# An attention and FFN kernel whose VectorE transposes start two pairs earlier, with twice as many pairs on float32 scores

## The chip, the cores and the metric

The kernel runs on one core of a Trainium2 chip. The metric is the device time of one launch in microseconds; the kernel before has a median of 1023.87 us over three runs (1023.54 to 1024.44). Five engines work side by side, each through its own queue in order: TensorE (PE, with its weight loads as PEld), VectorE (DVE), ScalarE (ACT), GpSimd (POOL) and SyncE (SP), which issues most DMAs. Matmuls write to eight PSUM banks.

## The reference

Attention with a decay over 8 batches, 8 heads, 576 positions and 64 dimensions, then a two-matrix feed-forward block over the 4608 tokens:

```python
scores = (q @ k.T) / 8                       # per batch and head, 576 x 576
cum    = cumsum(log(clip(f, 1e-4, 1)))       # 64 rows of 576
scores = where(causal, -1e9, scores + cum[:, None] - cum[None, :])
attn   = softmax(scores); o = attn @ v       # float32
h      = x @ w_in                            # x: 4608 x 512, w_in: 512 x 2048
g      = max(h, 0) + alpha * min(h, 0)
out    = g @ w_out                           # 2048 x 512
```

The term of a row's own position drops out of the softmax, so only the row of column sums, times -8, is added to the raw scores before the scaling by -1/8.

## The kernel before, in words

Two heads of a batch make a pair; there are 32 pairs, four to a batch. `attention(n)` writes down the work of pair n: loads, scores of four query tiles of 128 and a tail of 64 (heads on the two halves of TensorE's rows), a reduction on VectorE that adds the decay rows Z and takes the row's least value, an exponential on ScalarE, a transposition, the product with v (`values`), and the division by the sums (`rest`), which leaves x of the pair in two parts.

Scores come in two forms (`terms` in `load_n`). A pair below `NN` multiplies q and k in float32, one matmul for each piece. A later pair first splits q and k into a high and a low part (two copies on ScalarE, subtractions on POOL) and adds three products: Qh Kh, Qh Kl, Ql Kh.

Transposition also comes in two forms. A pair below `NX[0]` has its exponentials turned on TensorE in blocks of 128 against `ident` (L612), and ScalarE or VectorE carries them from PSUM to SBUF. A "turned" pair, from `NX[0]` on, has its exponentials laid out so that four VectorE transposes of 128 x 768 (L807) and 16 DMAs of 96 KB turn them; its k columns and its Z are permuted for that. The turned pairs use other cuts of the same SBUF (`big`, `wr`), which `swap` hands over.

Work that is not attention fills in: `load_w_in(fc)` turns one of 16 column groups of w_in into a high and a low part (`split64`: a square on ScalarE, L359, L360, L363 and L364 on VectorE in a scratch tile from the ring `rwa`, a copy on ScalarE, and two subtractions on POOL, L369), and `ffn1(b)` multiplies x of batch b with the 16 groups, 12 matmuls of 512 columns for each (all through the helper at L373), of which six need the first two pairs of the batch and six the other two. The rest of the first matrix and then the second one follow the last pair.

The order on each engine is set when the program is built. `op` records every step with an engine, a duration by a formula, a key, its dependencies and the buffers that it takes; `Plan.run` places them one by one at the earliest time that its own clock gives, lower keys first. So a table of constants moves instructions everywhere. Where the plan expects TensorE to stand, it puts matmuls of `ident` that nobody reads (`fill`, L470); a row of dummy matmuls on `wr` (L436) opens the program.

Of the kernel before, what the change touches and what calls it, by code (L numbers as in the profile page):

```python
# [18 lines left out]
NP = H // 2  # L19
# [7 lines left out]
NN = 4  # L27
# [7 lines left out]
NX = (10, B * NP)  # L35
# [14 lines left out]
LATE = (0, B - 1, B)  # L50

# [47 lines left out]
class Plan:  # L99
    def __init__(self):  # L100
        self.now = dict.fromkeys(ENGS, 0.0)
        self.chan = 0.0
        self.ops = []
        self.banks = self.fill = None

    def op(self, eng, ns, fn, key, deps=(), bufs=(), two=False, kb=0.0, glue=0.0, need=None):
        o = Op()
        o.glue, o.need = glue, need
        o.eng, o.ns, o.fn, o.key, o.bufs, o.two, o.kb = eng, ns / 1000.0 * SLACK.get(eng, 1.0), fn, key, bufs, two, kb
# [104 lines left out]
def attention_moe(  # L214
# [49 lines left out]
    rS, rT = Ring(banks, 2, 4), Ring(banks, 1, 3)  # L264
# [3 lines left out]
    rhs = Ring(Store([hs[:, i] for i in range(4)]))  # L268
# [16 lines left out]
    rT1 = Ring(Store(cuts_of(0, 3, 384)))  # L285
    re3, re = Ring(Store(cuts_of(1664, 1, 1024))), Ring(Store(cuts_of(2688, 3, S)))
# [5 lines left out]
    res = Ring(Store(cuts_of(1152, 2, 256) + [wf[:, 2560 + 256 * i : 2816 + 256 * i] for i in range(2)]))  # L292
# [9 lines left out]
    rwa = Ring(Store([wf[:, 2048:2560].bitcast(U32)]))  # L302
# [129 lines left out]

    o_wbf = op("DVE", 300, lambda: ve.memset(wbf, 1.0), -102)
    bw = Buf(rS)
    for i in range(7):
        op("PE", 800, lambda: [pe.matmul(bw.t, wbf[:, 0:128], wbf, start=True, stop=True) for _ in range(3)], -200, [o_wbf], [bw])  # L436
# [38 lines left out]
    def load_n(n, held):  # L475
# [5 lines left out]
        q_, k_ = (lambda: bqk.t[:, 0:QW]), (lambda: bqk.t[:, QW : QW + S])  # L481
        kq = -99 if first else -59 if n == 1 else kl
# [7 lines left out]
        Z, Zt = (lambda: bZ.t[0]), (lambda: bZ.t[1])  # L490
        rz = []
# [9 lines left out]
        for h in range(2):  # L501
            if spread:
                got = [zz]
            elif first:
                bz_ = Buf(rH)
                up = op("PE", 4 * c_mm(512), lambda h=h, bz_=bz_: mm(bz_.t, row()[:, h], ft()[:, 0:512], True, True), -60 + h, o_8 + [o_row], [bft, brow, bz_])
                got = [op("ACT", c_act(512), lambda h=h, bz_=bz_: ac.activation(Z()[:, h, 0:512], bz_.t, AF.Copy), -60, [up], [bz_, bZ])]
            else:
                c8_, o_ = (c8p, o_c8p) if n >= NX[0] else (c8, [o_c8])
                got = [op("SP", 400, lambda h=h, c8_=c8_: sy.dma_start(Z()[:, h, 0:512], c8_[bh + h : bh + h + 1, 0:512].broadcast_to([128, 512])),  # L510
                          kl + 1, o_, [bZ], kb=256)]
            if n >= NX[0]:
# [11 lines left out]
            tb = lambda k: tri.rearrange("p (k s) -> p k s", k=1).broadcast_to([128, k, 128])  # L524
            on, o_e, o_c = (ve, "DVE", c_dve) if first and h < FD else (po, "POOL", c_po)
# [3 lines left out]
            rz.append([m1, m2, m3])  # L529
        if spread:  # L530
            tz = [zt]
        elif first:
            bz2 = [Buf(rH), Buf(rH)]
            cut = ((0, 512), (512, S))

            def up2():
                for b_, (a0, a1) in zip(bz2, cut):
                    mm(b_.t[:, 0 : a1 - a0], row()[:, 2], ft()[:, a0:a1], True, True)

            up = op("PE", 4 * c_mm(512) + 440, up2, -58, o_8 + [o_row], [bft, brow] + bz2)  # L540
# [22 lines left out]
    waiting, behind, tails, later_x, quick_ops, value_ops = [], [], [], [], [], []  # L563

    def attention(n):
# [9 lines left out]
        turned = NX[0] <= n < NX[1]  # L575
        bv = Buf(rvr)
# [46 lines left out]
        def tail(st):  # L623

            nonlocal e4
            bt = bE if turned else Buf(re)
# [19 lines left out]
            if turned:  # L646
# [125 lines left out]
        def tile(h, i, st, bS, s, c0):  # L772

            nonlocal e4
            w = 128 * i + 128
# [25 lines left out]
            if turned:  # L801
# [12 lines left out]
                return  # L814
            if i == 1:
# [6 lines left out]
                t = op("PE", 3 * 109, tr1, st + 0.3, [be[h][0][1], nm, o_id], [bT, be[h][0][0], b1])  # L822
                e1[h] = evac(bT, 384, st + 0.3, [t], lambda: bT1[h].t, lambda: bT.t[:, :384], [bT1[h]])
            if i >= 2:
# [8 lines left out]
                t = op("PE", (i + 1 + last) * 109, tr2, st + 0.3, [nm, o_id] + ([nt] if last else []), [bT, b1] + ([bt] if last else []))  # L833
                to, tb = ((lambda: bT3.t[:, :, 192 * h : 192 * h + 128]), bT3) if i == 3 else ((lambda: bT2[h].t[:, 0:3, 0:128]), bT2[h])
# [48 lines left out]
        def rest():  # L883
            bx, xo = Buf(rx), []
# [38 lines left out]
        behind.append(values)  # L923
        if n == B * NP - 1:
# [3 lines left out]
        if n < NE - 1 or n in (NX[0] - 1, B * NP - 1):  # L928
            while behind:
                vb, vp, vd, done = behind.pop(0)()  # L930
                value_ops.append(op("PE", ns_v + 250, vp, k0 + 9.6 - hurry, vd, vb))
                done(value_ops[-1])
        if n >= NV2 and n % 2 == 0:
# [10 lines left out]
        elif not (n >= NV2 and n % 2 == 0):  # L944
# [3 lines left out]
            del later_x[:-keep]  # L948

# [65 lines left out]
    o_ct = [op("POOL", c_po(S) + 60, lambda h=h: sides(h), kc_ + 3, [o_cq]) for h in range(2)]  # L1015
    def swap():
        rS.most, rT.least, rH.most = 8, 0, 3
        for st, t in [(rE.store, big[:, 0:EW]), (rTT.store, big[:, EW + 3072 :]), (rTT.store, wf[:, 0:3072])] + [(rM.store, t) for t in cuts_of(EW, 4, 768)]:
            st.free.append((plan.t, len(st.items)))
            st.items.append(t)  # L1020

    op("-", 0, swap, 0, [value_ops[-1]] + [o for v in w_ready.values() for o in v])
# [300 lines left out]
```

## Time and profile before

| what | value |
|---|---|
| median of three runs | 1023.87 us (1023.54 to 1024.44) |
| profiled execution | 1022.34 us, its span 1020.5 us |
| busy in the span: PE, DVE, ACT, POOL | 1008.1, 803.6, 652.2, 389.5 us |
| mean granted TensorE clock | 0.998 of 2.4 GHz |
| chain of waits, share of PE | 94% |

The span runs from the first to the last instruction of one profiled execution. Busy times overlap, since the engines work side by side. A matmul's own time includes its way through the array, so the spacing of starts, not the mean duration, tells what one costs in a row of them.

### The profile page before, as it was taken

The page shows a single profiled execution, that of the slowest core. Times are in us where ns is not written, and L with a number is a line of the kernel's source. Part 1 is how long each engine was busy: PE and PEld are TensorE (multiplying, and loading weights), DVE is VectorE, ACT ScalarE, POOL GpSimd, SP SyncE. Part 2 cuts the span into 40 slices and gives each one's busy share as a digit, 9 for nine tenths or more (in the row PEclk, how much of TensorE's full clock was granted, in tenths as well). Part 3 has the DMA queues.
Part 4 walks back from the last instruction along what each step waited for, and adds up shares of the span by engine and source line. Part 5 has one row for each costly group of instructions (what it writes and reads, how often), then busy time and mean ns, then how long its engine had stood idle before and what let it go on. Part 6 is the DMA issues. An engine that isn't in the chain of part 4 may idle for free.

```text
span 1020.5 us, 22569 instructions
## 1 busy us (share of the span) xinstructions
PE 1008.1 (99%) x7932; PEld 889.0 (87%) x7932; DVE 803.6 (79%) x1727; ACT 652.2 (64%) x1550; POOL 389.5 (38%) x652
## 2 busy tenths in 40 slices
PE   9989989999999999999999999999999999999998
PEld 5778868888888888888888888899999999999998
DVE  6778875888887887857727976698998888989994
ACT  6979977677777777767634755555464645546551
POOL 6597983769877879758240000000000000000000
PEclk9999999999999999999999999999999999999999
DMA  6868764688888897887746674543443343434411
GB/s 197 245 187 264 241 192 124 184 229 263 264 256 250 240 260 217 257 239 208 203 140 222 208 232 164 196 146 125 134 134 126 124 145 125 136 113 145 131 57 42
DMA packets 126398, 187.88 MB, mean 184 GB/s; under 512 B 22135, under 2 KB 71790, under 8 KB 126286
## 3 DMA queue, kind: packets, MB, share of 16 engines
q1 hardware_dynamic: 121774, 173.27, 55.4%
q0 software_dynamic: 4224, 12.98, 4.8%
q8 instruction: 62, 1.02, 0.4%
q14 instruction: 50, 0.41, 0.1%
q10 hardware_dynamic: 288, 0.20, 0.1%
HBM read 102.95 MB, written 48.67 MB: 149 GB/s over the span
## 4 chain that ended last, share of the span: by engine, by line
PE 94%; POOL 3%; DVE 1%; DMA 1%; ACT 1%; issue 0%; SPq 0%; DVEq 0%; POOLq 0%
PE bank L373 90%; PE bank L612 2%; POOL wi L369 1%; PE bank L436 1%; DMA wr<-in_w_in_dram 1%; DMA ri<-rd 0%; PE bank L470 0%; POOL Z L519 0%; POOL Ql L558 0%; POOL Kl L558 0%; POOL xx L895 0%; DVE xs L891 0%; ACT big L608 0%; PE bank L691 0%; PE bank L651 0%
## 5 line engine op out<-in xcount | busy, mean ns | idle before, releaser
L373 PE MATMUL bank<-xx,wi 128*128 128x512 f32 x1728 | 410.5, 393 | 5.6 <-POOL wi L369 4.1
L373 PEld LDWEIGHTS bank<-xx,wi 128*128 128x128 f32 x1728 | 320.3, 188 | 74.7 <-POOL wi L369 5.0
L599 ACT ACTIVATE big<-big,st 128x384 f32<-128x384 f32 (+4 forms) x268 | 156.1, 585 | 22.2 <-DVE st L795 21.6
L795 DVE CUSTOM_DVE_ANT_0 big<-bank,Z 128x256 f32<-128x256 f32 (+3 forms) x211 | 92.2, 491 | 47.1 <-PE bank L373 42.6
L373 PE MATMUL bank<-wot,xx 128*128 128x256 f32 x1008 | 123.9, 283 | 0.0
L373 PE MATMUL bank<-wi,xx 128*128 128x256 f32 x1008 | 123.9, 283 | 0.0
L373 PEld LDWEIGHTS bank<-wi,xx 128*128 128x128 f32 x1008 | 122.3, 192 | 0.0
L373 PEld LDWEIGHTS bank<-wot,xx 128*128 128x128 f32 x1008 | 122.3, 192 | 0.0
L981 DVE SCALAR_TENSOR_TENSOR hs<-bank,sa,hs 128x512 f32<-128x512 f32 x96 | 71.6, 746 | 51.7 <-ACT hs L979 50.0
L979 ACT ACTIVATE hs<-bank,ab 128x512 f32<-128x512 f32 x96 | 65.9, 686 | 58.3 <-PE bank L373 56.6
L519 POOL TENSOR_TENSOR Z<-Z,tri 128x128 f32<-128x128 f32 x176 | 72.4, 443 | 46.5 <-DVE Z L497 42.5
L807 DVE STREAM_TRANSPOSE big<-big 128x768 f32<-128x768 f32 x88 | 81.1, 953 | 3.5 <-ACT big L599 3.5
L1207 ACT ACTIVATE xx<-gx 128x1024 fp32r<-128x1024 f32 x48 | 50.8, 1058 | 30.7 <-PE bank L373 13.4
L895 POOL TENSOR_TENSOR xx<-xs,xx 128x256 fp32r<-128x256 f32 x64 | 49.6, 792 | 47.5 <-ACT xx L893 47.0
L1210 DVE TENSOR_TENSOR xx<-gx,xx 128x1024 fp32r<-128x1024 f32 x48 | 58.5, 1219 | 7.9 <-ACT xx L1207 7.9
L373 PE MATMUL bank<-big,vr 128*64 128x128 f32 (+2 forms) x1136 | 62.7, 263 | 0.5 <-DVE st L640 0.3
L373 PE MATMUL bank<-wi,gh 128*128 128x256 f32 x504 | 62.4, 283 | 0.0
L373 PE MATMUL bank<-wot,gh 128*128 128x256 f32 x504 | 62.4, 283 | 0.0
L373 PEld LDWEIGHTS bank<-wot,gh 128*128 128x128 f32 x504 | 61.4, 192 | 0.1
L373 PEld LDWEIGHTS bank<-wi,gh 128*128 128x128 f32 x504 | 61.3, 192 | 0.0
L373 PEld LDWEIGHTS bank<-big,vr 128*64 128x64 f32 x1136 | 54.5, 137 | 7.9 <-issue 5.0
L373 PE MATMUL bank<-Kh,Qh 64*128 64x128 f32 (+2 forms) x280 | 58.7, 350 | 0.0
(161 smaller groups left out, 1747.9 us busy)
## 6 DMA issues: line engine op xcount, KB each, us to landing
hd<-hs SPq DMA_DIRECT2D x144, 256.0 KB, 3.9
wx<-hd SPq DMA_DIRECT2D x47, 512.0 KB, 3.4
rqk<-in_qk_dram SPq DMA_DIRECT2D x28, 512.0 KB, 6.1
hr<-hd SPq DMA_DIRECT2D x25, 512.0 KB, 4.7
big<-big SPq DMA_DIRECT2D x110, 96.0 KB, 2.8
wr<-big SPq DMA_DIRECT2D x110, 96.0 KB, 4.4
vr<-in_vv_dram SPq DMA_DIRECT2D x32, 320.0 KB
wr<-in_w_in_dram SPq DMA_DIRECT2D x16, 512.0 KB, 5.8
```

What stands on the lines that cost most here:

```text
L369: return [op("POOL", c_po(256), lambda h=h: po.tensor_tensor(wlo()[:, h], a()[:, h].bitcast(F32), whi()[:, h].bitcast(F32), ALU.subtract), ...
L373: pe.matmul(o, lhsT, rhs, start=start, stop=stop)
L519: ms.append(op("POOL", c_po(128), lambda to=to, i=i, zd=zd: po.tensor_tensor(to()[:, :, -1:], zd()[:, :, i : i + 1], tk(), ALU.add), kc + ...
L599: ex = op("ACT", c_exp(w), lambda: ac.activation(at(bt.t), at(bt.t), AF.Exp, bias=lo()[:, col : col + 1], scale=-1.0, accum_out=su()[:, co ...
L612: pe.transpose(t[:, c : c + 128], src[:, 128 * j : 128 * j + 128], ident)
L795: ve.tensor_tensor_reduce(out=o if turned else blk(o), in0=blk(bS.t[:, c0 : c0 + w]), in1=in1(), scale=-0.125, scalar=3.0e38, op0=ALU.add, ...
L807: tn = op("DVE", c_tr(768), lambda k=k: ve.transpose(part(bm[k].t), part(bE.t[:, 768 * k : 768 * k + 768])), k0 + TK + k / 10, done, [bE, ...
L895: xl = op("POOL", c_po(256), lambda r=r, t0=t0: po.tensor_tensor(bx.t[:, 1, t0 : t0 + 256], bxs[r].t[:, 0:256], bx.t[:, 0, t0 : t0 + 256]. ...
L979: cp = op("ACT", c_act(512), lambda bh=bh, bs=bs, fc=fc: ac.activation(bs.t, bh.t, AF.Relu, scale=ab[:, fc : fc + 1]), -1000, [last, o_sg] ...
L981: cp = op("DVE", c_dve(512), lambda bh=bh, bs=bs, fc=fc: ve.scalar_tensor_tensor(bs.t, bh.t, sa[:, fc : fc + 1], bs.t, ALU.mult, ALU.add), ...
L1207: his.append(op("ACT", c_acs(128 * GW * (j1 - j0)), lambda j0=j0, j1=j1, src=src, o_=o_: ac.activation(o_(0, j0, j1), src(), AF.Copy), key ...
L1210: rdy.append(op("DVE", c_dve(128 * GW * (j1 - j0)), lambda j0=j0, j1=j1, src=src, o_=o_: ve.tensor_tensor(o_(1, j0, j1), src(), o_(0, j0, ...
```

## The change

- `NX` starts at 8 instead of 10: pairs 8 and 9 become turned ones. Their Z is still loaded by DMA.
- `NN` is 8 instead of 4: pairs 4 to 7 take the float32 scores and are no longer split.
- The decay rows of the pairs that are not turned are kept in another arrangement, so that two additions of 256 columns for each head stand where an addition of 384, one of 128 and a copy of 128 stood. For pair 0 the two additions of one head read PSUM.
- The rows that are spread for pair 0 are the sums themselves, with -8 in the selecting matrix, instead of sums that VectorE has multiplied by -8. The selecting matrix has a place of its own (`rT1`) and is written earlier on POOL.
- Six of the 21 opening matmuls go.
- The score ring keeps four banks from the start and may hold six (two and four before).
- The scratch ring `rwa` of the w_in conversion has two tiles; the second is a fourth of `hs`, which `ffn1` gets back after the last conversion.
- SBUF is handed to the turned pairs in three steps (`swap`, `swap1`, `swap2`): after the last TensorE transposition, after the last value product before them, and after the last conversion. Other cuts of `big` move to suit.
- A table `SHIFT`, which is empty, could add to the keys.

```diff
-NN = 4
+NN = 8
-NX = (10, B * NP)
+NX = (8, B * NP)
...
-    rS, rT = Ring(banks, 2, 4), Ring(banks, 1, 3)
+    rS, rT = Ring(banks, 4, 6), Ring(banks, 1, 3)
...
-    rhs = Ring(Store([hs[:, i] for i in range(4)]))
+    rhs = Ring(Store([hs[:, i] for i in range(3)]))
...
-    rwa = Ring(Store([wf[:, 2048:2560].bitcast(U32)]))
+    rwa = Ring(Store([wf[:, 2048:2560].bitcast(U32), hs[:, 3].bitcast(U32)]))
...
-    brow = Buf(re)
+    brow = Buf(rT1)
...
-                po.affine_select(o, o, pattern=[[0, w]], base=-h, channel_multiplier=1, compare_op=ALU.not_equal, fill=1.0)
-
-    o_row = op("POOL", 1500, rows, -100, (), [brow])
+                po.affine_select(o, o, pattern=[[0, w]], base=-h, channel_multiplier=1, compare_op=ALU.not_equal, fill=-8.0)
+
+    o_row = op("POOL", 1000, rows, -101, (), [brow])
...
-    for i in range(7):
+    for i in range(5):
...
-                up = op("PE", 4 * c_mm(512), lambda h=h, bz_=bz_: mm(bz_.t, row()[:, h], ft()[:, 0:512], True, True), -60 + h, o_8 + [o_row], [bft, brow, bz_])
+                up = op("PE", 4 * c_mm(512), lambda h=h, bz_=bz_: mm(bz_.t, row()[:, h], cu()[:, 0:512], True, True), -60 + h, o_sc + [o_row], [bcu, brow, bz_])
...
-            m1 = op(o_e, o_c(128 * 3), lambda z4=z4, on=on: on.tensor_tensor(z4()[:, 6:9], z4()[:, 0:3], tb(3), ALU.add), kc + 0.1, got + [o_mask], [bZ])
-            m2 = op(o_e, o_c(128), lambda z4=z4, on=on: on.tensor_tensor(z4()[:, 3], z4()[:, 3], tri, ALU.add), kc + 0.2, got + [o_mask], [bZ])
-            m3 = op(o_e, o_c(128) / 2, lambda z4=z4, on=on: on.tensor_copy(z4()[:, 4], z4()[:, 1]), kc + 0.2, got, [bZ])
+            if first and h < FD:
+                s4 = lambda bz_=bz_: bz_.t.rearrange("p (j s) -> p j s", s=128)
+                m1 = op("DVE", c_dve(256), lambda z4=z4, s4=s4: ve.tensor_tensor(z4()[:, 3:7:3], s4()[:, 0:2], tb, ALU.add), kc + 0.1, [up, o_mask], [bz_, bZ])
+                m2 = op("DVE", c_dve(256), lambda z4=z4, s4=s4: ve.tensor_tensor(z4()[:, 2:6:3], s4()[:, 2:4], tb, ALU.add), kc + 0.2, got + [o_mask], [bz_, bZ])
+            else:
+                m1 = op("POOL", c_po(256), lambda z4=z4: po.tensor_tensor(z4()[:, 3:7:3], z4()[:, 0:2], tb, ALU.add), kc + 0.1, got + [o_mask], [bZ])
+                m2 = op("POOL", c_po(256), lambda z4=z4: po.tensor_tensor(z4()[:, 2:6:3], z4()[:, 4:6], tb, ALU.add), kc + 0.2, got + [o_mask], [bZ])
...
-    op("-", 0, swap, 0, [value_ops[-1]] + [o for v in w_ready.values() for o in v])
+    o_swap = op("-", 0, swap, 0, turn_ops)
+    o_swap = op("-", 0, swap1, 0, [value_ops[-1], o_swap])
+    op("-", 0, swap2, 0, [o_swap] + [o for v in w_ready.values() for o in v])
```

What that does to the order is shown at three places. A row is the line, the instruction, and what it writes and reads, with the tiles' numbers.

First TensorE, right behind the opening matmuls. `rqk0` holds q and k of pair 0, `big_109` the sums and the selecting matrix. Before:

```order
L373 MATMUL bank2_79<-rqk0_102 128x256
L373 MATMUL bank3_80<-rqk0_102 128x384
L373 MATMUL bank4_81<-rqk0_102 128x384
L470 MATMUL bank5_82<-ident_123 128x128 x6
L373 MATMUL bank5_82<-big_109 128x512
L373 MATMUL bank6_83<-big_109 128x512
L373 MATMUL bank7_84<-big_109 128x512
```

And of the change, the same place:

```order
L378 MATMUL bank2_79<-rqk0_102 128x256
L378 MATMUL bank3_80<-big_109 128x512
L378 MATMUL bank4_81<-big_109 128x512
L378 MATMUL bank5_82<-rqk0_102 128x384
L378 MATMUL bank6_83<-rqk0_102 128x384
L378 MATMUL bank7_84<-big_109 128x512
L378 MATMUL bank0_77<-big_109 128x64
```

The spreading of pair 0's sums moves ahead of the scores of 384 columns, and the six filling matmuls are gone.

Second VectorE, at two conversions of w_in that follow each other closely; `ISA` on `big` and `st` are reductions of scores. Before:

```order
L359 TENSOR_SCALAR wr_110<-wr_110 128x512
L360 SCALAR_TENSOR_TENSOR wr_110<-wr_110 128x512
L363 SCALAR_TENSOR_TENSOR wr_110<-wr_110 128x512
L364 SCALAR_TENSOR_TENSOR wr_110<-wi_88,wr_110 128x512
L795 ISA big_109,st1_114<-bank4_81,Z0_104 128x384
L795 ISA st1_114 128x1
L359 TENSOR_SCALAR wr_110<-wr_110 128x512
L360 SCALAR_TENSOR_TENSOR wr_110<-wr_110 128x512
```

And of the change, at about the same conversions:

```order
L364 TENSOR_SCALAR wr_110<-wr_110 128x512
L365 SCALAR_TENSOR_TENSOR wr_110<-wr_110 128x512
L368 SCALAR_TENSOR_TENSOR wr_110<-wr_110 128x512
L369 SCALAR_TENSOR_TENSOR wr_110<-wi_88,wr_110 128x512
L826 ISA big_109,st1_114<-bank1_78,Z0_104 128x384
L826 ISA st1_114 128x1
L364 TENSOR_SCALAR hs_93<-wr_110 128x512
L365 SCALAR_TENSOR_TENSOR hs_93<-wr_110,hs_93 128x512
```

The second of the two now writes to `hs`, so it does not have to wait for POOL to be done with the scratch of the first.

Third TensorE in pair 8; `xx,wi` are matmuls of `ffn1`, `ident` with `big` are transposes, `Kh0`, `Qh0` and so on the split parts of pair 8. Before:

```order
L373 MATMUL bank0_77<-Kh0_96,Ql0_95 128x512
L373 MATMUL bank5_82<-xx_89,wi_88 128x512 x6
L612 MATMUL bank7_84<-ident_123,big_109 128x128 x3
L831 MATMUL bank7_84<-ident_123,big_109 64x128
L612 MATMUL bank1_78<-ident_123,big_109 128x128 x3
L373 MATMUL bank5_82<-xx_89,wi_88 128x512 x6
L373 MATMUL bank4_81<-Kh0_96,Qh0_94 128x256
```

And of the change:

```order
L378 MATMUL bank6_83<-Kl0_97,Qh0_94 128x320
L378 MATMUL bank6_83<-Kh0_96,Ql0_95 128x320
L378 MATMUL bank4_81<-xx_89,wi_88 128x512 x12
L378 MATMUL bank1_78<-xx_89,wi_88 128x512 x12
L378 MATMUL bank7_84<-xx_89,wi_88 128x512 x6
L674 MATMUL bank0_77<-ident_123,big_109 64x128
L378 MATMUL bank2_79<-Kh1_100,Qh1_98 128x128
```

All scores of the pair now stand in one piece, followed by 30 matmuls of `ffn1`, and one transpose of the tail is left of the pair's 25.

## Rows read from the trace of the kernel before

**Rows 1.** The page: busy us (share of the span) x instructions.
```profile
PE 1008.1 (99%) x7932; PEld 889.0 (87%) x7932; DVE 803.6 (79%) x1727; ACT 652.2 (64%) x1550; POOL 389.5 (38%) x652
```

**Rows 2.** Windows: stretch, length, busy by engine, granted clock, DMA share, GB/s.
```profile
1.47:60.87 59.40, 58.50 (x522) 41.39 (x522) 44.20 (x146) 47.87 (x145) 38.21 (x76) 1.00 0.81 232
60.87:171.76 110.89, 104.87 (x865) 85.13 (x864) 81.47 (x186) 91.66 (x245) 89.11 (x125) 0.98 0.66 201
171.76:524.33 352.57, 352.38 (x2957) 292.55 (x2956) 270.15 (x661) 253.00 (x725) 253.78 (x435) 1.00 0.80 231
524.33:1020.50 496.17, 492.36 (x3596) 469.92 (x3594) 407.30 (x734) 258.92 (x436) 7.60 (x10) 1.00 0.44 142
```

**Rows 3.** Timeline of PE at its gaps: start, us, instructions, idle before and releaser.
```profile
68.14 2.11 PE L373 MATMUL bank<-xx,wi 128*128 128x512 f32 x8 [1.16 <-POOL wi L369]
71.46 0.73 PE L373 MATMUL bank<-xx,wi 128*128 128x512 f32 x2 [1.21 <-POOL xx L895]
...
146.08 0.73 PE L373 MATMUL bank<-xx,wi 128*128 128x512 f32 x2 [0.29 <-ACT wi L368]
149.80 1.19 PE L373 MATMUL bank<-xx,wi 128*128 128x512 f32 x4 [2.98 <-POOL wi L369]
```

**Rows 4.** Windows, right behind the last of those gaps.
```profile
150.80:154.40 3.60, 3.60 (x13) 2.82 (x11) 3.50 (x6) 0.69 (x2) 2.75 (x4) 0.53 0.92 290
```

**Rows 5.** Waits of DVE from 20 to 172 us: total, times, longest.
```profile
DVE wr L359 <- POOL wi L369: 16.3, 9, 3.5
```

**Rows 6.** Windows: three pairs turned on TensorE, then three turned on VectorE.
```profile
82.10:132.32 50.22, 49.95 (x436) 41.10 (x435) 42.17 (x100) 46.70 (x127) 45.42 (x62) 1.00 0.83 250
217.16:259.10 41.94, 41.74 (x378) 35.04 (x377) 35.11 (x89) 33.08 (x96) 35.43 (x63) 1.00 0.84 242
```

**Rows 7.** Windows, instructions on wi alone: the same stretches, and one dense run.
```profile
82.10:132.32 50.22, 25.08 (x96) 17.11 (x96) 6.82 (x8) 9.20 (x15) 10.21 (x14) 1.00 0.83 250
217.16:259.10 41.94, 23.96 (x102) 18.95 (x102) 0.00 (x0) 0.00 (x0) 0.00 (x0) 1.00 0.84 242
174.78:181.61 6.83, 6.83 (x30) 5.44 (x30) 0.00 (x0) 0.00 (x0) 0.00 (x0) 1.00 0.24 86
```

**Rows 8.** The page: the VectorE transposes of the turned pairs.
```profile
L807 DVE STREAM_TRANSPOSE big<-big 128x768 f32<-128x768 f32 x88 | 81.1, 953 | 3.5 <-ACT big L599 3.5
```

**Rows 9.** Chain of waits, the float32 scores of pairs: start, us, what.
```profile
27.32 0.86 PE bank L373 x8
...
29.96 0.84 PE bank L373 x4
...
31.50 0.97 PE bank L373 x4
...
37.07 1.06 PE bank L373 x4
```

**Rows 10.** Timeline of PE: the first of 30 matmuls of pair 10's scores.
```profile
171.76 0.33 PE L373 MATMUL bank<-Kh,Qh 64*128 64x128 f32 x2
```

**Rows 11.** Timeline of the start.
```profile
6.03 1.46 PE L436 MATMUL bank<-wr 128*128 128x512 bf16 x6
...
6.46 0.68 DVE L400 TENSOR_SCALAR big<-big 64x256 f32<-64x256 f32 x2 [0.20 <-ACT warm L393]
...
10.46 3.01 PE L373 MATMUL bank<-big 64*128 64x512 f32 x8
...
11.62 0.60 ACT L507 ACTIVATE Z<-bank 128x512 f32<-128x512 f32 x1 [5.18 <-PE bank L373]
...
13.13 0.28 DVE L795 CUSTOM_DVE_ANT_0 big<-bank,Z 128x128 f32<-128x128 f32 x1
```

**Rows 12.** The page, DMA issues: queue, count, KB each, us to landing.
```profile
hd<-hs SPq DMA_DIRECT2D x144, 256.0 KB, 3.9
...
wr<-in_w_in_dram SPq DMA_DIRECT2D x16, 512.0 KB, 5.8
```

**Rows 13.** Last step of the conversions: count, min/median/max ns, first and last start.
```profile
L369 POOL TENSOR_TENSOR wi<-wr,wi x32: 721/737/1044, 39.7 to 155.6; 128x256 fp32r<-128x256 f32 x32
```

More of the change, by code (lines that the diff above doesn't have):

```diff
@@ L104, in __init__, with at @@
         self.banks = self.fill = None
+        self.shift = 0.0
+    def at(self, kind, n):
+        self.shift = SHIFT.get((kind, n), 0.0)
     def op(self, eng, ns, fn, key, deps=(), bufs=(), two=False, kb=0.0, glue=0.0, need=None):
@@ L108, in op @@
         o.glue, o.need = glue, need
-        o.eng, o.ns, o.fn, o.key, o.bufs, o.two, o.kb = eng, ns / 1000.0 * SLACK.get(eng, 1.0), fn, key, bufs, two, kb
+        o.eng, o.ns, o.fn, o.key, o.bufs, o.two, o.kb = eng, ns / 1000.0 * SLACK.get(eng, 1.0), fn, key + self.shift, bufs, two, kb
         o.outs, o.ready, o.end, o.n = [], 0.0, None, 0
@@ L291, in attention_moe @@
     wf = wr.bitcast(F32)
-    res = Ring(Store(cuts_of(1152, 2, 256) + [wf[:, 2560 + 256 * i : 2816 + 256 * i] for i in range(2)]))
+    res = Ring(Store(cuts_of(2752, 2, 256) + [wf[:, 2560 + 256 * i : 2816 + 256 * i] for i in range(2)]))
     G0 = 2 * NZ
@@ L427, in rows @@
             for o, w in ((row()[:, h], 128), (row()[:, 2, 64 * h : 64 * h + 64], 64)):
-                po.affine_select(o, o, pattern=[[0, w]], base=-h, channel_multiplier=1, compare_op=ALU.not_equal, fill=1.0)
-    o_row = op("POOL", 1500, rows, -100, (), [brow])
+                po.affine_select(o, o, pattern=[[0, w]], base=-h, channel_multiplier=1, compare_op=ALU.not_equal, fill=-8.0)
+    o_row = op("POOL", 1000, rows, -101, (), [brow])
     o_wbf = op("DVE", 300, lambda: ve.memset(wbf, 1.0), -102)
     bw = Buf(rS)
-    for i in range(7):
-        op("PE", 800, lambda: [pe.matmul(bw.t, wbf[:, 0:128], wbf, start=True, stop=True) for _ in range(3)], -200, [o_wbf], [bw])
+    for i in range(5):
+        op("PE", 1290 if i < 3 else 650, lambda: [pe.matmul(bw.t, wbf[:, 0:128], wbf, start=True, stop=True) for _ in range(3)], -200, [o_wbf], [bw])
     def select():
@@ L490, in load_n @@
         Z, Zt = (lambda: bZ.t[0]), (lambda: bZ.t[1])
+        if n >= NX[0]:
+            z_raw = lambda h: Z()[:, h, 0:512]
+            two_ = lambda t: t
+        else:
+            z_raw = lambda h: Z()[:, h, 0:1024].rearrange("p (a x) -> p a x", x=512)[:, :, 0:256]
+            two_ = lambda t: t.rearrange("p (a x) -> p a x", x=256)
         rz = []
@@ L501, in load_n @@
         for h in range(2):
+            plan.at("D", n)
             if spread:
@@ L523, in load_n @@
             z4 = lambda h=h: Z()[:, h, 0:1152].rearrange("p (j s) -> p j s", s=128)
-            tb = lambda k: tri.rearrange("p (k s) -> p k s", k=1).broadcast_to([128, k, 128])
-            on, o_e, o_c = (ve, "DVE", c_dve) if first and h < FD else (po, "POOL", c_po)
-            m1 = op(o_e, o_c(128 * 3), lambda z4=z4, on=on: on.tensor_tensor(z4()[:, 6:9], z4()[:, 0:3], tb(3), ALU.add), kc + 0.1, got + [o_mask], [bZ])
-            m2 = op(o_e, o_c(128), lambda z4=z4, on=on: on.tensor_tensor(z4()[:, 3], z4()[:, 3], tri, ALU.add), kc + 0.2, got + [o_mask], [bZ])
-            m3 = op(o_e, o_c(128) / 2, lambda z4=z4, on=on: on.tensor_copy(z4()[:, 4], z4()[:, 1]), kc + 0.2, got, [bZ])
-            rz.append([m1, m2, m3])
+            tb = tri.rearrange("p (k s) -> p k s", k=1).broadcast_to([128, 2, 128])
+            if first and h < FD:
+                s4 = lambda bz_=bz_: bz_.t.rearrange("p (j s) -> p j s", s=128)
+                m1 = op("DVE", c_dve(256), lambda z4=z4, s4=s4: ve.tensor_tensor(z4()[:, 3:7:3], s4()[:, 0:2], tb, ALU.add), kc + 0.1, [up, o_mask], [bz_, bZ])
+                m2 = op("DVE", c_dve(256), lambda z4=z4, s4=s4: ve.tensor_tensor(z4()[:, 2:6:3], s4()[:, 2:4], tb, ALU.add), kc + 0.2, got + [o_mask], [bz_, bZ])
+            else:
+                m1 = op("POOL", c_po(256), lambda z4=z4: po.tensor_tensor(z4()[:, 3:7:3], z4()[:, 0:2], tb, ALU.add), kc + 0.1, got + [o_mask], [bZ])
+                m2 = op("POOL", c_po(256), lambda z4=z4: po.tensor_tensor(z4()[:, 2:6:3], z4()[:, 4:6], tb, ALU.add), kc + 0.2, got + [o_mask], [bZ])
+            rz.append([m1, m2])
+        plan.at("D", n)
         if spread:
@@ L537, in up2 @@
                 for b_, (a0, a1) in zip(bz2, cut):
-                    mm(b_.t[:, 0 : a1 - a0], row()[:, 2], ft()[:, a0:a1], True, True)
-            up = op("PE", 4 * c_mm(512) + 440, up2, -58, o_8 + [o_row], [bft, brow] + bz2)
+                    mm(b_.t[:, 0 : a1 - a0], row()[:, 2], cu()[:, a0:a1], True, True)
+            up = op("PE", 4 * c_mm(512) + 440, up2, -58, o_sc + [o_row], [bcu, brow] + bz2)
             tz = [op("ACT", c_act(a1 - a0), lambda b_=b_, a0=a0, a1=a1: ac.activation(Zt()[:, a0:a1], b_.t[:, 0 : a1 - a0], AF.Copy), -58, [up], [b_, bZ])
@@ L561, in load_n @@
         return out, rz, rt, bZ, [(Qh, Kh), (Qh, Kl), (Ql, Kh)]
-    waiting, behind, tails, later_x, quick_ops, value_ops = [], [], [], [], [], []
+    waiting, behind, tails, later_x, quick_ops, value_ops, turn_ops = [], [], [], [], [], [], []
     def attention(n):
@@ L774, in tile @@
             nonlocal e4
+            plan.at("A", n)
             w = 128 * i + 128
@@ L814, in tile @@
                 return
+            plan.at("T", n)
             if i == 1:
@@ L883, in rest @@
         def rest():
+            plan.at("X", n)
             bx, xo = Buf(rx), []
@@ L948, in attention @@
             del later_x[:-keep]
+        plan.at("", 0)
     w_ready = {}
@@ L1015, in attention_moe, with more, swap1, swap2 @@
     o_ct = [op("POOL", c_po(S) + 60, lambda h=h: sides(h), kc_ + 3, [o_cq]) for h in range(2)]
+    def more(store, *items):
+        for t in items:
+            store.free.append((plan.t, len(store.items)))
+            store.items.append(t)
     def swap():
         rS.most, rT.least, rH.most = 8, 0, 3
-        for st, t in [(rE.store, big[:, 0:EW]), (rTT.store, big[:, EW + 3072 :]), (rTT.store, wf[:, 0:3072])] + [(rM.store, t) for t in cuts_of(EW, 4, 768)]:
-            st.free.append((plan.t, len(st.items)))
-            st.items.append(t)
-    op("-", 0, swap, 0, [value_ops[-1]] + [o for v in w_ready.values() for o in v])
+        more(rE.store, big[:, 0:EW])
+    def swap1():
+        more(rM.store, *cuts_of(EW, 4, 768))
+        more(rTT.store, big[:, EW + 3072 :])
+    def swap2():
+        more(rTT.store, wf[:, 0:3072])
+        more(rhs.store, hs[:, 3])
+    o_swap = op("-", 0, swap, 0, turn_ops)
+    o_swap = op("-", 0, swap1, 0, [value_ops[-1], o_swap])
+    op("-", 0, swap2, 0, [o_swap] + [o for v in w_ready.values() for o in v])
     for n in range(NX[0], B * NP):
```

36 lines of the change are left out of this document (29 added, 7 removed).

## The prediction

> **What bounds the kernel now.** I began with the share of each engine: TensorE is busy for 1008.1 of 1020.5 us and no other engine for more than 79% [rows 1]. So an edit is worth what it takes off TensorE's own work, or what it takes off the time in which TensorE stands. Second I cut the span at three of TensorE's landmarks: its first matmul (1.47 us), the first matmul of the FFN (60.87) and the first score of pair 10, the first turned pair (171.76); the last value product ends at 524.33 [rows 2]. In the third and fourth stretch TensorE stands for hardly any time until the last few microseconds (352.38 of 352.57 busy in the third). In the second it stands for 110.89 - 104.87 = 6.0 us and its mean clock is 0.98. In the first it is rarely idle, but dummy and filling matmuls count as busy there, and ScalarE is the fullest real worker, 47.87 of 59.40 us. Third I looked at what TensorE does at the second stretch's gaps [rows 3]: 1.16 and 1.21 us near 70 us, in the first FFN block, and 0.29 and 2.98 us from 146 on, where FFN matmuls wait for the low half of w_in from POOL. Right behind that wait the granted clock is 0.53 for 3.6 us, so nearly all of it at the lower level, 1.2 GHz [rows 4]; that loses 3.6 x (1 - 0.53) = 1.7 us. Last I asked who holds the conversions of w_in up: VectorE stood 16.3 us, nine times, at the first step of a conversion until POOL had finished the one before [rows 5]. That is the one scratch tile.
>
> **Part 1, pairs 8 and 9 turned on VectorE.** Three pairs turned on TensorE last from 82.10 to 132.32, three turned on VectorE from 217.16 to 259.10, both from value product to value product [rows 6]. They hold 96 and 102 FFN matmuls, and one costs 6.83 / 30 = 0.228 us in a row of them [rows 7]. Without these a pair takes (50.22 - 21.9) / 3 = 9.45 us in the first form and (41.94 - 23.2) / 3 = 6.24 in the second. Two pairs: -6.4 us of TensorE. Against it VectorE gets eight transposes of 0.953 us [rows 8], 7.6 us in all, and SP and POOL 32 more DMA issues. These are hidden: with all of that VectorE is busy for 35.11 of 41.94 us in three turned pairs, and TensorE for 41.74 [rows 6].
>
> The Trainium skill ("VectorE: DVE Perf Modes", Rules for kernel authors) says to transpose 128 x 128 on TensorE where a result in PSUM will do, and this kernel's values are copied out of PSUM, so the rule speaks against this part. By the rule the part would lose time; the rows say it gains 3.2 us a pair, because here it is TensorE that has no time left. The case in which VectorE would decide stands below as a rival.
>
> **Part 2, float32 scores for pairs 4 to 7.** One such pair takes four pieces of 0.86, 0.84, 0.97 and 1.06 us, 3.73 us together [rows 9]. The three split products of a pair take 3.02 us, from 171.76 [rows 10] to 174.78, where the run of 30 FFN matmuls starts [rows 7]. Four pairs: +2.8 us on TensorE (+2.0 if the split form costs a little more in three pieces than in one). ScalarE loses eight copies and POOL 24 subtractions, which the sum takes only as less queueing, in part 4.
>
> **Part 3, the start.** The last six opening matmuls take 1.46 us [rows 11], so the scores can begin up to 1.3 us sooner, if k of pair 0 has landed, which no row tells. In the new order the first sums are spread after four score matmuls (about 0.9 us by the pieces of 128 and 256) instead of at 10.46 [rows 11]: at 7.0 to 8.3 us. They don't wait for the multiplication by -8 any more, and the sums are there before VectorE begins it at 6.46. From the spreading to the first reduction it was 13.13 - 10.46 = 2.67 us; the addition from PSUM still waits for ScalarE's copy (11.62 for 0.60) in its second half, so I take 2.3. First reduction at 9.3 to 10.6 instead of 13.13: 2.5 to 3.8 us sooner. Pair 1 may not follow all the way, since its rows come through DRAM behind that same multiplication, whose time is not moved. I take -3.0, from -1.0 to -3.8; ScalarE's load up to the first FFN matmul is about the same, so the gain is carried there.
>
> **Part 4, the waits after 60.87.** The scratch wait of 16.3 us on VectorE goes with the second tile, and POOL, busy for 89.11 of 110.89 us in that stretch [rows 2], loses its subtractions for four pairs. So the low halves come sooner, the wait at 146 (0.29 + 2.98 us) goes and the low clock behind it (1.7): -5.0. The 2.4 us near 70 I leave as they are: pair 3's x still comes through POOL in order. What is late next: the second FFN block. It needs x of pairs 4 to 7, and in the new order its first matmuls stand right behind pair 9's scores, where before two more pairs lay ahead of them, and pair 7's division stands behind pair 8's transposes on VectorE. I take 2.0 us, the size of the first block's wait, between 0 and 5.
>
> **Edits at nothing.** The new layout of Z moves as many columns in fewer instructions on POOL, which is not waited for in the first pairs. Three instead of four tiles of `hs` while conversions run: a group of 12 FFN matmuls takes 2.7 us and a store 3.9 us to land [rows 12], so three tiles give 8.2 us for a copy and a store; without that cover each group would wait about 1 us. The banks only change which of several ready pieces goes first, and the three-step hand-over lets the turned pairs in sooner.
>
> **The sum.** -6.4 + 2.8 - 3.0 - 5.0 + 2.0 = -9.6 us. On the profiled execution (1022.34 us, 1.84 above its span) that is 1012.7. The median of the three runs is 1023.87, 1.53 above it, so 1014.3.
>
> **Rivals.**
> - The wait comes back at the new turning point. Pair 8 needs all of pair 7's transposes, and its values need 16 DMAs, while three conversions are still on their way. Then the 5.0 us stay: 1019.3. For it: both gaps of rows 3 are POOL's queue, which the builder's order did not foresee. Against it: POOL has less to do.
> - More goes: the second block does not wait, and the first block's 2.4 us vanish as well with lighter POOL and VectorE queues. -9.6 - 2.0 - 2.4 = -14.0: 1009.9.
> - Slower: the conversions keep their pace. Their last steps run from 39.7 to 155.6 us, 15 intervals of 7.7 us [rows 13]. In the new order two pairs (2 x 9.45) and 60 FFN matmuls (13.7) fewer stand before the turned pairs, so TensorE would come to the sixteenth column group at about 144 us: 171.76 - 3.0 - 5.0 + 2.0 - 18.9 - 13.7 + 2.8 = 136, then 3.0 of scores and 24 FFN matmuls (5.5). If that group is ready only at 156.4, TensorE stands for 12 us and loses the clock's 1.7 again: -9.6 - 2.0 + 12 + 1.7 = +2.1, 1026.0. It decides from a last conversion at about 154 on. For it: a load takes 5.8 us to land [rows 12], and there are still two load tiles. Against it: two loads in flight allow one conversion in some 5 us, and the 16.3 us of VectorE's waiting were the scratch tile's.
> - Slower as well: VectorE decides in pairs 8 and 9. Its 7.6 us come on top and the 6.4 don't go: +4.4, 1028.3. Against it stand the 35.11 of 41.94 us.
>
> **How the numbers follow.** Chances: forecast 0.48 (its own range 1010 to 1018), the wait's return 0.18, more goes 0.23, conversions keep their pace 0.08, VectorE decides 0.03. The range over all of these, with the bounds of parts 3 and 4 (-0.8 to +2.0 and -2.0 to +3.0) is 1006.5 to 1022.5. A measurement of this kernel tells 0.2%, 2.0 us, from no change. The forecast and "more goes" are faster in nearly all of their spread (0.70), the wait's return in 0.13 of its 0.18: faster 0.83; the rest of it and edges of the others make 0.06 for no change and 0.11 for slower.
>
> **What would show it.** Right: the first reduction at 9.3 to 10.6 us; the first FFN matmul near 58; no granted clock below 0.9 between 60 and 200 us; the last low half of w_in before 144; 24 turned pairs at 6.2 us beside their FFN matmuls; VectorE's wait for L369's successor well under 16 us. Wrong: a TensorE gap of over 3 us in or behind pair 8, waiting for w_in, x of pair 7, or the turned tiles of pair 8; a first FFN matmul later than 60; the last value product later than 515 in the span.

## The result, and the profile after

1007.95 us (median of 4 runs, 1006.64 to 1008.97) against 1023.7 for the kernel before in the same session: ratio 0.9846, 95% interval 0.9829 to 0.9863. 9.6 us less were forecast, 15.8 came. The time lies in the whole range (1006.5 to 1022.5), but below the forecast's own (1010 to 1018), and nearest to the rival "more goes" (1009.9). The profiled execution (1008.97, the slowest of the four) has a span of 1007.2, 13.3 below that of [rows 1]; what follows accounts for these 13.3, not for the 15.8 between the medians.

The page of the changed kernel, busy time by engine, answers to [rows 1]:
```profile
PE 999.4 (99%) x7828; PEld 878.8 (87%) x7828; DVE 804.5 (80%) x1730; ACT 643.4 (64%) x1534; POOL 371.7 (37%) x625
```
Windows at the same landmarks as [rows 2] (first FFN matmul, first score of the first turned pair, end of the last value product):
```profile
1.47:59.98 58.51, 57.15 (x493) 38.95 (x493) 46.69 (x149) 45.85 (x141) 32.64 (x63) 1.00 0.78 234
59.98:130.90 70.92, 70.89 (x544) 55.58 (x543) 58.64 (x131) 62.24 (x164) 46.80 (x59) 1.00 0.79 247
130.90:511.25 380.35, 378.99 (x3200) 314.35 (x3198) 291.23 (x717) 275.71 (x795) 283.77 (x489) 1.00 0.81 235
511.25:1007.20 495.95, 492.37 (x3596) 469.95 (x3594) 407.44 (x734) 258.89 (x436) 7.60 (x10) 1.00 0.44 142
```
The last stretch is as long as before (496.17). The first is 0.89 us shorter. All else lies between: 463.46 us before, 451.27 now. In the second and third stretch TensorE now stands for 0.03 and 1.4 us (6.0 and 0.2 before), and the mean granted clock is 1.00 in each.

Three pairs turned on VectorE, pairs 8 and 9 among them; then two pairs with float32 scores beside FFN work. In each fence the whole window, then the instructions on `wi` alone:
```profile
156.95:199.99 43.04, 43.04 (x384) 36.13 (x384) 37.00 (x91) 33.91 (x100) 34.45 (x61) 1.00 0.86 242
...
156.95:199.99 43.04, 25.50 (x108) 20.01 (x108) 0.00 (x0) 0.00 (x0) 0.00 (x0) 1.00 0.86 242
```
```profile
80.18:109.98 29.80, 29.80 (x250) 22.92 (x248) 24.28 (x64) 27.51 (x76) 15.96 (x23) 1.00 0.81 244
...
80.18:109.98 29.80, 13.31 (x48) 8.81 (x48) 3.74 (x5) 6.44 (x10) 8.04 (x11) 1.00 0.81 244
```
With the 0.228 us of an FFN matmul [rows 7], a turned pair takes (43.04 - 24.6) / 3 = 6.15 us of TensorE, a float32 pair (29.80 - 10.9) / 2 = 9.43. With split products it was 9.45 [rows 6].

The sum by these rows: turned pairs -6.6, float32 scores 0, start -0.9, standing and low clock from 7.7 to 1.4 us, so -6.3. Together -13.8, against -13.3 in the spans.

The only gap of TensorE over 0.3 us between 60 and 200 us, and VectorE's rows behind it (timeline):
```profile
149.31 0.41 PE L378 MATMUL bank<-Kh,Qh 128*128 128x320 f32 x1 [1.36 <-DVE st L826]
```
```profile
141.89 3.54 DVE L838 STREAM_TRANSPOSE big<-big 128x768 f32<-128x768 f32 x4
...
147.60 1.31 DVE L927 TENSOR_TENSOR xs<-xs,ri 128x256 f32<-128x256 f32 x2 [1.14 <-DMA ri<-rd]
148.84 0.41 DVE L826 CUSTOM_DVE_ANT_0 big<-bank,Z 128x256 f32<-128x256 f32 x1
```
TensorE waits there for a bank that the reduction at 148.84 frees. That one stood behind pair 7's division, which waited 1.14 us for its factors from DRAM: VectorE takes its list in order.

The start (timeline). The reduction began at 13.13 before [rows 11]:
```profile
10.00 0.28 DVE L826 CUSTOM_DVE_ANT_0 big<-bank,Z 128x128 f32<-128x128 f32 x1
...
42.89 0.94 DVE L364 TENSOR_SCALAR hs<-wr 128x512 uint32<-128x512 uint32 x1
43.87 1.10 DVE L365 SCALAR_TENSOR_TENSOR hs<-wr,hs 128x512 uint32<-128x512 uint32 x1
45.00 1.04 DVE L368 SCALAR_TENSOR_TENSOR hs<-wr,hs 128x512 uint32<-128x512 uint32 x1
46.15 0.98 DVE L369 SCALAR_TENSOR_TENSOR hs<-wi,hs 128x512 f32<-128x512 f32 x1
47.05 0.74 DVE L629 COPY big<-bank 128x256 f32<-128x256 f32 x2
```
The value products of the first four pairs begin at 20.6, 30.6, 41.1 and 55.6, before at 23.5, 33.1, 44.8 and 56.5. Of 3.7 us won, 2.8 go between the third and the fourth, where a conversion of 4.2 us now stands ahead of pair 3's copy at 47.05. The second tile is not what puts it there: in e3 below, with one tile, it stands in the same place (timeline), and pair 3's values begin at 56.9:
```profile
43.03 0.94 DVE L364 TENSOR_SCALAR wr<-wr 128x512 uint32<-128x512 uint32 x1
...
47.20 0.74 DVE L629 COPY big<-bank 128x256 f32<-128x256 f32 x2
```

### The profile page after: what moved, and what is told of

Same layout as the page of the kernel before. It is cut to its first block, busy times and chain, and to the rows that moved or that the text cites. A ratio compares the mean times of both kernels' runs of the same rounds, so it can differ in the third digit from the quotient of the medians.

```text
span 1007.2 us, 22383 instructions
## 1 busy us (share of the span) xinstructions
PE 999.4 (99%) x7828; PEld 878.8 (87%) x7828; DVE 804.5 (80%) x1730; ACT 643.4 (64%) x1534; POOL 371.7 (37%) x625
## 4 chain that ended last, share of the span: by engine, by line
PE 95%; DMA 2%; DVE 2%; ACT 1%; SPq 0%; issue 0%; DVEq 0%
PE bank L378 92%; PE bank L634 2%; DMA Z<-c8p 1%; DMA ri<-rd 1%; PE bank L441 1%; DMA rd<-R 0%; ACT big L620 0%; DVE xs L927 0%; PE bank L674 0%; DVE big L826 0%; DVE big L629 0%; PE bank L717 0%; SPq L730 0%; PE bank L475 0%; ACT big L630 0%
## 5 line engine op out<-in xcount | busy, mean ns | idle before, releaser
L826 DVE CUSTOM_DVE_ANT_0 big<-bank,Z 128x384 f32<-128x384 f32 (+1 forms) x220 | 93.0, 480 | 54.2 <-PE bank L378 45.6
L533 POOL TENSOR_TENSOR Z<-Z,tri 128x128 f32<-128x128 f32 x192 | 78.1, 437 | 44.8 <-DVE Z L509 35.7
L838 DVE STREAM_TRANSPOSE big<-big 128x768 f32<-128x768 f32 x96 | 88.6, 953 | 2.6 <-ACT big L620 2.5
L378 PEld LDWEIGHTS bank<-big,vr 128*64 128x64 f32 x1088 | 51.9, 137 | 9.2 <-issue 4.8
L378 PE MATMUL bank<-big,vr 128*64 128x128 f32 (+2 forms) x1088 | 59.7, 263 | 0.0
L1016 ACT ACTIVATE hs<-bank,sg 128x512 f32<-128x512 f32 x48 | 33.1, 689 | 41.2 <-PE bank L378 32.2
```

The costliest lines, as they stand in the source:

```text
L378: pe.matmul(o, lhsT, rhs, start=start, stop=stop)
L533: ms.append(op("POOL", c_po(128), lambda to=to, i=i, zd=zd: po.tensor_tensor(to()[:, :, -1:], zd()[:, :, i : i + 1], tk(), ALU.add), kc + ...
L826: ve.tensor_tensor_reduce(out=o if turned else blk(o), in0=blk(bS.t[:, c0 : c0 + w]), in1=in1(), scale=-0.125, scalar=3.0e38, op0=ALU.add, ...
L838: tn = op("DVE", c_tr(768), lambda k=k: ve.transpose(part(bm[k].t), part(bE.t[:, 768 * k : 768 * k + 768])), k0 + TK + k / 10, done, [bE, ...
L1016: cp = op("ACT", c_act(512), lambda bh=bh, bs=bs, fc=fc: ac.activation(bs.t, bh.t, AF.Copy, scale=sg[:, fc : fc + 1]), -1000, [last, o_sg] ...
```

## The experiments

All were timed beside the kernel before (1023.7 to 1024.2 in each session). "Ratio" is to that kernel, with its 95% interval. The changed kernel was timed only with its result, so differences to its 1007.95 go from one session to another. The first four take one part out of the changed kernel.

**One part out**

```
e1:  NX = (10, B * NP)            e2:  NN = 4
e3:  rwa = Ring(Store([wf[:, 2048:2560]...])), hs ring of 4
e4:  21 opening matmuls; fill=1.0 and ft() in place of -8.0 and cu()
```

> The changed kernel with VectorE turning only from the eleventh pair on, as before (NX = 10), all else as changed. Theory A (the 48 transposes that TensorE no longer makes for pairs 8 and 9, 0.109 us each, are the gain of part 1): 5.2 to 6.4 us slower than the changed kernel, 1013 to 1014.5 against 1007.95. Theory B (the turning point gives back what the transposes save, since TensorE waits 1.36 us there for VectorE's reductions behind the four transposes): 0 to 3 us slower, 1008 to 1011.

1013.67, ratio 0.9899 (0.9884 to 0.9914): 5.7 us slower than the changed kernel, theory A. TensorE stands nowhere between 127 and 200 us, so what this run loses is TensorE's own work: 6.6 us for two pairs by the rows above, less the 1.36 us for which only the changed kernel stands, 5.2.

> The changed kernel with float32 scores in pairs 0 to 3 only, as before (NN = 4), all else as changed. Theory A (a pair's float32 scores cost TensorE as much as its three split products, 3.1 us against 3.0 to 3.2, so part 2 moves TensorE by nothing): 1007 to 1009, and a little later if POOL's 24 subtractions delay w_in or x. The prediction's own term: 2.8 us faster, 1005. Theory C (the relief of POOL is what removed the waits in the conversions): 3 us or more slower, from 1011 on, with TensorE idle again for over 3 us between 60 and 160.

1029.83, ratio 1.0057 (1.0043 to 1.0070): 21.9 us slower, which theory C alone allows. TensorE stands for 5.3 and 8.0 us in these windows, and its mean granted clock falls to 0.89 and 0.86:
```profile
110.00:140.00 30.00, 24.73 (x150) 19.07 (x149) 24.05 (x48) 21.70 (x54) 22.55 (x27) 0.89 0.62 196
140.00:175.00 35.00, 27.04 (x184) 20.56 (x184) 26.99 (x62) 24.38 (x74) 28.58 (x52) 0.86 0.74 198
```
The conversions end later, too: the twelfth at 125.2 us, in the changed kernel at 108.1.

> The changed kernel with one scratch tile for the conversions of w_in and four tiles for what the FFN stores, as before, all else as changed. Theory A (the second tile is what removed the waits of TensorE for w_in, 6.0 us idle and 1.7 us at the low clock before): 5 to 8 us slower, 1013 to 1016, with VectorE's wait on POOL in the conversions back at over 10 us. Theory C (the lighter POOL removed them): 0 to 2 us slower, 1008 to 1010.

1019.59, ratio 0.9954 (0.9939 to 0.9970): 11.6 us slower, more than theory A. The last conversion ends at 151.4 us, in the changed kernel at 136.4, and VectorE's wait is back near its old size (16.3):
```profile
DVE wr L364 <- POOL wi L374: 14.9, 8, 3.2
```

> The changed kernel with the opening of before: 21 opening matmuls, and the first sums spread from the multiplied rows, all else as changed. Theory A (the 3 us won at the start are given back before the first FFN matmul, 59.98 against 60.87, because two conversions stand ahead of pair 3 on VectorE): 0.5 to 1.5 us slower, 1008.5 to 1009.5. The prediction's own term: 3 us slower, 1011.

1008.69, ratio 0.9860 (0.9838 to 0.9881), no difference that can be told (0.7 us; its runs go from 1007.57 to 1013.29). The first reduction comes at 11.20, so the new opening is worth 1.2 of the 3.1 us there, and the rest of the change 1.9. The first FFN matmul even stood at 57.66, before the 59.98 of the changed kernel.

**What NN = 8 and the second tile do, alone and apart**

```
e5:  scores split from pair 4 on; line 925 still tests n < 8
e6:  line 925 tests n < 4          e7:  before, NN = 8
e8:  before, rwa with hs[:, 3], hs ring of 3 until the hand-over
e10: before, hs ring of 3 until the hand-over
```

> The changed kernel with split products in pairs 4 to 7, but with the planner's rule for the division (line 925: no added lag of 2000 ns below pair NN) left at eight pairs. It parts the two things that NN sets, after e2_four came to 1029.83, 21.9 us above the changed kernel. Theory C (the work that the split form puts on POOL, 24 subtractions, and on ScalarE, 8 copies, makes TensorE wait for w_in and x): 15 to 25 us slower than the changed kernel, 1023 to 1033. Theory D (the other order of the divisions did it): within 5 us of it, 1006 to 1013.

1032.91, ratio 1.0088 (1.0073 to 1.0102): theory D falls, so the rule of line 925 is not the cause. The split form brings work and another order; this run does not part the two.

> The changed kernel with the float32 scores of eight pairs, but the planner's lag of 2000 ns for a division's factors from pair 4 on, as before, so that VectorE's multiplications of pairs 4 to 7 stand later in its queue. In the changed kernel VectorE waits twice for pair 7's factors from DRAM, 1.92 us before 140.09 and 1.14 us before 147.60, and TensorE waits 1.36 us at 149.31 for the reduction behind. Theory A (that queue is what is left of waits at the turning point): TensorE's idle time there under 0.4 us, 1 to 2 us faster, 1006 to 1007. Theory B (the order changes elsewhere and loses what it wins): 1007.5 to 1011.

1013.04, ratio 0.9894 (0.9880 to 0.9908), 5.1 us slower: theory B, and more than it said. TensorE stands for 2.5 us between 140 and 175.

> The kernel before with NN = 8 alone: float32 scores in pairs 4 to 7, and no other part of the change. Prediction's term: 2.8 us slower, 1026.5. Theory C (POOL's relief alone removes the waits for w_in, and the form costs TensorE nothing): 4 to 8 us faster, 1016 to 1020.

1019.09, ratio 0.9956 (0.9940 to 0.9973): 5.0 us faster alone. The prediction had this part as a cost of 2.8.

> The kernel before with the second scratch tile alone (taken from the four tiles of the FFN's stores and given back at the hand-over), and no other part of the change. Prediction's part 4: the wait at 146 and the low clock behind it go, 5 us faster, 1019. Theory C (without POOL's relief the queue of POOL takes the place of the scratch tile): within 2 us of 1024, VectorE's wait on POOL under 5 us but TensorE still idle over 3 us between 60 and 172.

1032.16, ratio 1.0081 (1.0068 to 1.0093): 8.1 us slower, against both theories. VectorE's wait for POOL falls from 16.3 to 2.7 us, but TensorE waits for x and w_in through POOL, and VectorE for TensorE (timeline, then VectorE's waits from 20 to 172 us):
```profile
74.63 2.83 PE L373 MATMUL bank<-xx,wi 128*128 128x512 f32 x8 [3.57 <-POOL xx L895]
...
115.07 2.07 PE L373 MATMUL bank<-xx,wi 128*128 128x512 f32 x4 [2.12 <-POOL wi L369]
```
```profile
DVE big L795 <- PE bank L373: 17.2, 7, 5.6
DVE hs L359 <- POOL wi L369: 2.7, 2, 1.4
```

> The kernel before with one scratch tile, but three instead of four tiles for what the FFN stores, until the hand-over; nothing else of the change. It parts the two things that e8_before_two_tiles (1032.16) changed at once. Theory F (the second scratch tile itself does harm while POOL is full): 1023 to 1025, as before. Theory G (the lost store tile does it): 1029 to 1033.

1023.87, ratio 1.0000 (0.9989 to 1.0012): the lost store tile costs nothing in the kernel before. The 8.1 us come with the second scratch tile.

**Is it POOL's queue?**

```
e9:  pairs 4 to 7 float32, and also per pair:
     2 x ac.activation(bQ.t[j], raw(), AF.Copy)
     6 x po.tensor_tensor(bQ.t[j + 1][..], raw()[..], .., ALU.subtract)
e12: the same without the six subtractions
```

> The changed kernel, whose scores of pairs 4 to 7 stay float32 on TensorE; but ScalarE's 8 copies and POOL's 24 subtractions of the split form are still made, into tiles that no one reads, and the scores do not wait for them. Theory C (POOL's queue is what part 2 relieves; TensorE's form does not matter): 10 to 25 us slower than the changed kernel, 1018 to 1033, with POOL busy for over 38 of the 50 us from 60 to 110 (30.5 in the changed kernel). Theory E (the scores' own wait for the subtractions is the loss, not the queue): 1008 to 1012.

1024.27, ratio 0.9999 (0.9987 to 1.0010), 16.3 us slower; POOL 41.00 of 50 us. That looked like theory C, though the work itself and the order that it brings are not parted here either.

> As e9_idle_splits, but POOL's 24 subtractions are left out and only ScalarE's 8 copies of the split form are still made into tiles that no one reads. Theory C (it is POOL's queue, not ScalarE's): 1007 to 1010, within 2 us of the changed kernel, POOL busy for about 30.5 of the 50 us from 60 to 110 as in the changed kernel. Theory H (ScalarE's copies do it): 1020 to 1025, as e9_idle_splits with 1024.27.

1027.25, ratio 1.0036 (1.0022 to 1.0050): theory C falls. The time lies above the range of theory H as well, and the load on the engines does not explain it: from 60 to 110 us POOL is busy for less time than in the changed kernel and ScalarE for hardly more. First this run, then the changed kernel:
```profile
60.00:110.00 50.00, 49.44 (x350) 37.25 (x349) 40.48 (x92) 44.90 (x116) 28.35 (x35) 1.00 0.75 236
```
```profile
60.00:110.00 50.00, 49.97 (x357) 38.14 (x356) 43.80 (x106) 44.37 (x121) 30.47 (x39) 1.00 0.79 243
```
But for the first (48.4 us against 42.2), the conversions end hardly later either: from 2.7 us sooner to 1.7 later. The last steps of those in the second tile, in this run and in the changed kernel (count, min/median/max ns, first and last start):
```profile
L374 POOL TENSOR_TENSOR wi<-hs,wi x16: 727/740/1187, 49.1 to 133.1; 128x256 fp32r<-128x256 f32 x16
```
```profile
L374 POOL TENSOR_TENSOR wi<-hs,wi x16: 726/744/981, 48.7 to 135.7; 128x256 fp32r<-128x256 f32 x16
```
What differs is the order of TensorE's list (timeline of this run, pair 7's scores):
```profile
111.42 0.59 PE L378 MATMUL bank<-rqk 128*128 128x256 f32 x2
111.66 9.91 PE L378 MATMUL bank<-xx,wi 128*128 128x512 f32 x42
121.41 0.70 PE L378 MATMUL bank<-rqk 128*128 128x320 f32 x2
...
129.94 1.85 PE L378 MATMUL bank<-xx,wi 128*128 128x512 f32 x4 [1.84 <-POOL wi L374]
131.72 1.65 PE L378 MATMUL bank<-rqk 64*128 64x384 f32 x4
```
```profile
103.25 0.60 PE L378 MATMUL bank<-rqk 128*128 128x256 f32 x2
103.50 3.13 PE L378 MATMUL bank<-xx,wi 128*128 128x512 f32 x12
106.79 0.70 PE L378 MATMUL bank<-rqk 128*128 128x320 f32 x2
...
109.14 0.92 PE L378 MATMUL bank<-rqk 64*128 64x384 f32 x4
```
The second fence is the changed kernel: 12 FFN matmuls between the first two of these pieces, where e12 has 42. FFN matmuls counted in the list ahead of pair 6's value product, its start, and the time, for the changed kernel, the kernel before, and the runs in which pair 6 comes late:

| kernel | FFN matmuls | start | us |
|---|---|---|---|
| changed | 102 | 110.0 | 1007.95 |
| before | 108 | 114.5 | 1023.7 |
| e7 | 132 | 120.2 | 1019.09 |
| e2 | 144 | 129.5 | 1029.83 |
| e9 | 168 | 134.5 | 1024.27 |
| e12 | 174 | 133.3 | 1027.25 |
| e5 | 180 | 137.5 | 1032.91 |
| e8 | 192 | 146.6 | 1032.16 |

The count alone does not rank the times: e7 with 132 is faster than the kernel before with 108, and e3, with 72 and a start at 102.2, took 1019.59.

In all five that lie above 1024 the list draws FFN matmuls ahead of pair 7's last scores; TensorE then runs into columns of w_in that are not converted, and stands, while VectorE waits for those scores. For e12, VectorE's waits for scores (us in all, times, longest), and the window behind:
```profile
DVE big L830 <- PE bank L378: 9.6, 3, 8.3
```
```profile
140.00:175.00 35.00, 29.04 (x183) 21.28 (x182) 22.18 (x55) 21.43 (x65) 16.45 (x33) 0.80 0.57 154
```
The waits for w_in are only a part: TensorE stands for 10.2 us between 60 and 175 us (1.4 in the changed kernel), 3.7 of them for w_in; most of the rest comes after 152 us, in waits for ScalarE. Besides, the granted clock is 0.50, the lower level, from 130.2 to 133.6 and from 157.5 to 171.1, right behind such waits; TensorE is busy there for 13.8 us, which costs half of that, 6.9. Together, 8.8 us of longer standing and 6.9, that is 15.7 of the 18.4 us between the two spans.

That the list starts it, and not load, rests on e12 alone; no run kept its copies with the changed kernel's list. In e2 and e9 the conversions themselves end up to 17.1 and 11.1 us later, so load may play its part there. Which entry makes the builder turn the list over stays open.

**Pair 3 first**

```
e11: b1 of w_in's second conversion also depends on VectorE's evacuations of pair 3
```

> The changed kernel, with the second conversion of w_in (its first step on VectorE at 42.89) made to wait for VectorE's evacuations of pair 3, so that pair 3 stands ahead of it in VectorE's queue. Theory A (this conversion is what takes back the start's gain, 3.7 us at pair 2's values but 0.9 at the first FFN matmul): pair 3's values 2 to 3 us sooner, the first FFN matmul near 57.5, and the end 1.5 to 3 us sooner, 1005 to 1006.5. Theory B (the conversions are then late for the FFN matmuls or for the turning point, and take it back there): 1007 to 1010.

1014.23, ratio 0.9896 (0.9879 to 0.9913), 6.3 us slower: the conversion only moved in front of pair 3's last reductions, and TensorE waits there:
```profile
60.65 4.11 PE L380 MATMUL bank<-big,vr 128*64 128x128 f32 x44 [3.83 <-DVE st L666]
```
So it does not test what it was to test: what eats the start's gain between the third and the fourth pair stays open. No version beat the changed kernel.

## Why the prediction was right, and where not

Set beside the sum by the rows (-13.8), the sum of the prediction (-9.6) took too little by 0.2 in part 1, 2.8 in part 2 and 3.3 in part 4, and too much by 2.1 at the start. So it is partly luck that it came this near: one error offset others. The rival "more goes" came within 2 us with +2.8 and -3.0 still in it, which nearly cancel. The range "over all of these" holds neither of the two slower rivals (1026.0 and 1028.3).

- **Part 1** was right: -6.4 forecast, -6.6 by the rows, 5.7 by e1. VectorE, 37.00 of 43.04 us busy, hides the transposes. The Trainium skill ("VectorE: DVE Perf Modes", Rules for kernel authors) would transpose 128 x 128 on TensorE where a result in PSUM will do; here that form was 5.7 us slower (e1), and the measurement decides.
- **Part 2** failed in sign. TensorE's +2.8 came from pieces of the opening [rows 9], 3.73 us for the 20 matmuls of a pair. Beside FFN work in the changed kernel such 20 take 3.11 us, counted from one start to the next (between 80.2 and 110.0), and the 30 split ones before take 3.1 to 3.3, so the form costs about 0. Why they are slower in the opening no run tells. What the sum "takes only as less queueing" was the larger half: alone the part gives 5.0 us (e7), and without it the changed kernel is 21.9 slower (e2). But POOL's queue is not shown to be the reason, since e12 loses 19.3 without the subtractions.
- **Part 3**: the first reduction came at 10.00, inside 9.3 to 10.6, but "the gain is carried there" failed: -0.9 at the first FFN matmul, and nothing at the end that e4 can tell. The opening gave only 1.2 of the 3.1 us (e4).
- **Part 4** was right that the scratch wait, the wait at 146 and the low clock go, and e3 shows the second tile's share. That a lighter POOL does the rest is not shown (e12). It was wrong on the second FFN block (2.0 forecast, no wait) and on the 2.4 us near 70, which went as well. New is the 1.36 us at 149.31. The prediction had named pair 7's division there, behind pair 8's transposes and for x; it waits for its factors from DRAM instead, and holds up a bank.
- The promised marks: last low half of w_in at 135.7 (before 144), a granted clock of 1.00 from 60 to 200 us, turned pairs at 6.15 us, no wait of VectorE on the scratch tile, last value product over at 511.25 (before 515). The first FFN matmul, 59.98, is nearer to "wrong" (60) than to 58.
- **What the sum could not hold:** its terms are not additive. The second tile is worth 11.6 us in the changed kernel (e3) and costs 8.1 in the one before (e8). That each part re-sorts the whole list is the likely reason; no run held the list fixed.

## What to carry to other kernels

Where a builder sorts the instructions from estimates, a part's worth depends on the others: time it alone and left out before calling it a gain. A second buffer that takes one wait away can cost more than it saves (e8); where the list then draws dependent work ahead of its data, look there first. Price an operation from rows of the stage where it will stand.

## What the hardware showed unexpectedly

- VectorE's 128x512 `scalar_tensor_tensor` steps on integers (L365, L368) took 0.68 to 0.70 us in all 14 cases of the changed kernel that lay for under a third of their time beside a POOL tensor operation (11 of them beside none), and 0.89 to 1.18 in 15 of the 18 that lay for over half of it beside one; the steps at 43.87 (1.10 us) and 45.00 are two of these.
- Beside FFN work a pair took TensorE no longer with float32 scores (9.43 us with all that is not FFN) than with three split products (9.45).
